# A fused attention and feed-forward kernel: two queues for a batch's stores, a divided last transpose, and another order of the last part's additions

## The chip, the cores and the metric

The kernel runs on one core of a Trainium2 chip. The metric is the device time of one execution in microseconds (us), given as the median of several executions of the same program. Beside these times stands one profiled execution, with a trace of every engine: PE (TensorE) does the matmuls and transposes, DVE (VectorE) and ACT (ScalarE) the element-wise work and the copies out of PSUM, POOL (GpSimd) little here, and SP only issues transfers (DMAs). ACT can issue transfers as well, from the same stream of instructions that holds its copies.

## The reference

Two steps. The first is attention whose mask comes from a hash; the second is a feed-forward layer with a parametric ReLU.

```python
# q, k, v: (4, 8, 768, 64); proj: (64, 6)
q_bucket = sum((q @ proj > 0) * 2**arange(6)); k_bucket = likewise
mask   = q_bucket[..., :, None] == k_bucket[..., None, :]
scores = where(mask, q @ k.T / sqrt(64), -1e9)
attn   = softmax(scores) @ v
x = attn.transpose(0, 2, 1, 3).reshape(3072, 512)
# moe_w_in: (512, 2048), moe_w_out: (2048, 512), moe_alpha: (2048,)
h = x @ moe_w_in
g = maximum(h, 0) + alpha * minimum(h, 0)
out = g @ moe_w_out            # (3072, 512) float32
```

## The kernel before

**Two paths.** `fast_path` computes everything under assumptions on the size of the inputs. `verdict()` tests these on the chip and writes an integer `flag`; after `fast_path` every engine reads the flag and branches over `general_path`, which is not run here (L401 and L402 in the profile, and L1245 for the program's closing waits).

**Stages.** The first third of the span is attention, unit by unit. After it come the feed-forward products for the four batches `b` = 0 to 3, as a list of 15 blocks per batch: eight blocks `ff1` (names `f_0` to `f_7`: x times w_in, with the parametric ReLU) and seven blocks `ff2` (names `z_p` for `p` in `ORDER = (1, 2, 5, 6, 3, 7, 4)`: the seven products of a fast matrix product of the Strassen kind that makes g times w_out). The result of `ff2` is in the tiles `m`, written `m_1` to `m_7` here; sums of them are the four parts of the batch's output, the parts 2, 3, 5 and 4 in the order in which they are ready.

**A block.** Each block is again seven small products, in the class `Product`. They go into three PSUM banks, a, b and c. `step(n)` emits one product and what follows it. Two products add into bank a after the bank was copied out, so that ACT's copy `keep` (L861 in the profile, tiles `..p` and `..u`) must have read the bank before PE writes it again. The four quarters of a block's result are "11", "12", "22" and "21"; `finish` puts each into the tile m: an addition on DVE (L990), or, for "21", a copy on ACT (L996). In block 4, the last of a batch, `finish` also adds `m_1`: for three quarters by a second addition (`add`, L984), for "21" by an addition straight from PSUM (L994).

**Order.** The order on every engine is the order in which the program emits the instructions; `do` keeps the compute instructions so, and each engine works through its own instructions in order. Around the end of a batch the block loop emits: the sums that prepare the next block's operands (`sum_g2`, L972, tile `gs`; `sum_w2`, L964, tile `ws`), `turn_out()`, then the next block's `step(1)`, and only then `step(4)` of the block at hand.

**Output.** The tiles `m` are transposed against the output. `turn_out` does this for finished parts: two DVE transposes of 32x32 blocks (L1014) into a tile `o`, then twelve stores of 32 KB each (L1020), all on SP's queue. For the two last parts of the last batch, `turn_last(0)` (part 5) and `turn_last(1)` (part 4) use PE transposes of 128x128 (L1036), which they call cells `(t, i)`: column block `t` of 3, row half `i` of 2. ACT copies them out of PSUM (L1041) and the stores are L1042: part 5 in one store on SP's queue, part 4 in two on ACT's. In part 4 the second store needs the quarter "21", which comes last.

**The verdict.** `largest()` leaves four maxima for each partition in the tile `top`. `verdict()` turns its four columns by four PE transposes into one row (L1056), reduces that row to four numbers (L1057), and computes the flag from them in seven small DVE instructions.

Of the kernel before, what the change touches and what calls it, by code (L numbers as in the profile page):

```python
# [8 lines left out]
F32 = mybir.dt.float32  # L9
# [3 lines left out]
ALU = mybir.AluOpType  # L13
# [335 lines left out]
def kernel(  # L349
# [48 lines left out]
    keep = ctx.enter_context(tc.tile_pool(name="keep", bufs=1))  # L398
    flag = keep.tile([1, 1], mybir.dt.int32, name="flag")
    fast_path(*args, flag)  # L400
    again = tc.nc.values_load(flag[0:1, 0:1])  # L401
    with tc.If(again > 0):  # L402
# [4 lines left out]
def fast_path(  # L407
# [12 lines left out]
    nc = tc.nc  # L420
    P = 128
    B, H, S, D = q.shape
# [8 lines left out]
    CH = 3  # L431
# [5 lines left out]
    SAFE = (40.0 / SCALE) ** 2  # L437
    EPS = 1e-30
    HI_MIN = 2.0 ** -15
    HI_END = 2.0  # L440

    do = tc.keep_in_program_order
    PE, DVE, ACT, POOL = nc.tensor, nc.vector, nc.scalar, nc.gpsimd

    const = ctx.enter_context(tc.tile_pool(name="const", bufs=1))
    dram = ctx.enter_context(tc.tile_pool(name="dram", bufs=1, space=bass.MemoryType.DRAM))
    mid = ctx.enter_context(tc.tile_pool(name="mid", bufs=2))
    psum = ctx.enter_context(tc.tile_pool(name="ps", bufs=1, space=bass.MemoryType.PSUM))
# [9 lines left out]
    ident = const.tile([P, P], F32, name="ident")  # L458
# [99 lines left out]
    order, left = [], [list(range(HW)), list(range(HW, NW))]  # L558
# [104 lines left out]
    def two_banks(name):  # L663
        return psum.tile([P, 2, 512], F32, name=name, tag="sc", bufs=3)
# [170 lines left out]
    class Product:  # L835

        def __init__(self, name, width, nk, left, right, finish):
            self.name, self.width, self.nk = name, width, nk  # L840
            self.left, self.right, self.finish = left, right, finish
            self.ps, self.sb = {}, {}

# [20 lines left out]
        def step(self, n):  # L864
            if n == 1:
                self.times("a", 0, 0, True)
                self.keep("a", "p1")
            elif n == 2:
                self.times("b", 1, 1, True)
            elif n == 22:  # L870
                self.finish("11", self.sb["p1"], self.ps["b"])
            elif n == 5:
                self.times("c", 3, 3, True)
                self.keep("c", "p5")
            elif n == 6:
                self.times("a", 4, 4, False)
                self.keep("a", "u1")
            elif n == 3:
                self.times("c", 6, 2, False)
                self.finish("12", self.sb["u1"], self.ps["c"])  # L880
            elif n == 7:
                self.times("a", 5, 5, False)
                self.keep("a", "u2")
                self.finish("22", self.sb["p5"], self.sb["u2"])
            elif n == 4:
                self.times("a", 2, 6, False)
                self.finish("21", self.ps["a"], None)
# [32 lines left out]
    H2, HK, HC = DM // 4, NI // 2, CW // 2  # L920
    w2, g2, m2, to_turn = {}, {}, {}, []
# [52 lines left out]
    def ff2(b, n):  # L974

        p = ORDER[n]
        acc = late[0].tile([P, 2, CW], F32, name=f"m{b}_{p}", tag={1: "m1", 5: "m5"}.get(p, "m"), bufs=1 if p in (1, 5) else 3)
        m2[b, p] = acc

        def add(to, x, *quarter):  # L980
            t, x = m2[b, to], m2[b, x]
            if quarter:
                t, x = (a[:, quarter[0], quarter[1] * HC : (quarter[1] + 1) * HC] for a in (t, x))
            do(DVE.tensor_tensor(t, t, x, op=ALU.add))  # L984

        def finish(c, x, more):
            i, jj = int(c[0]) - 1, int(c[1]) - 1
            dst = acc[:, i, jj * HC : (jj + 1) * HC]
            if more is not None:
                do(DVE.tensor_tensor(dst, x, more, op=ALU.add))  # L990
                if p == 4:
                    add(4, 1, i, jj)
            elif p == 4:
                do(DVE.tensor_tensor(dst, x, m2[b, 1][:, i, jj * HC : (jj + 1) * HC], op=ALU.add))  # L994
            else:
                do(ACT.copy(dst, x))  # L996
            if c == "21":

                for to, x in {2: [(2, 1)], 6: [(1, 6)], 3: [(3, 5), (3, 1)], 7: [(1, 7), (5, 1)]}.get(p, []):
                    add(to, x)  # L1000
                done = {2: (2, 0, 0), 3: (3, 0, 1), 7: (5, 1, 1), 4: (4, 1, 0)}.get(p)
                if done:
                    to_turn.append((b, *done))

        return Product(
            f"z{b}_{p}", HC, HK, lambda m, k: w2[b, n, m][:, k], lambda m, k: g2[b, n, m][:, k], finish,
        )

    def turn_out():
        while to_turn:  # L1010
            b, p, half, ch = to_turn.pop(0)
            o = late[0].tile([P, CW, 2], F32, name=f"o{b}_{p}", tag="o")
            for i in range(2):
                do(DVE.transpose(o[:, :, i], m2[b, p][:, i]))  # L1014

            src = o.rearrange("p (c w d) i -> p c w (d i)", c=CH, d=32)
            for a in range(DM // 128):
                for c in range(CH):
                    cols = slice(half * DM // 2 + 64 * a, half * DM // 2 + 64 * a + 64)
                    nc.sync.dma_start(  # L1020
                        out_v[b, ch * CH + c].rearrange("(w r) d -> r w d", r=32)[:, :, cols],
                        src[32 * a : 32 * a + 32, c],
                    )

    def turn_last(n):

        b, p, half, ch = to_turn.pop(0)
        o = late[0].tile([P, CH, P, 2], F32, name=f"o_{p}", tag=("o", "m5")[n], bufs=2 - n)
        dst = out_v[b, ch * CH : (ch + 1) * CH].rearrange("c p d -> p c d")[:, :, half * 2 * P : (half + 1) * 2 * P]
        goes = [([(t, i) for i in range(2) for t in range(CH)], slice(0, CH))]  # L1030
        if n:
            goes = [([(2, 0), (2, 1), (0, 0), (1, 0)], slice(2, CH)), ([(0, 1), (1, 1)], slice(0, 2))]
        for cells, ts in goes:
            ps = two_banks(f"to{p}").rearrange("p a f -> p (a f)").rearrange("p (i t f) -> p i t f", i=2, f=P)
            for t, i in cells:
                do(PE.transpose(ps[:, i, t], m2[b, p][:, i, t * P : (t + 1) * P], ident))  # L1036
            for i in range(2):
                t = [c[0] for c in cells if c[1] == i]
                if t:
                    t = slice(min(t), max(t) + 1)  # L1040
                    do(ACT.copy(o[:, t, :, i], ps[:, i, t]))  # L1041
            (nc.scalar if n else nc.sync).dma_start(dst[:, ts], o[:, ts].rearrange("p t f i -> p t (f i)"))  # L1042


    top = const.tile([P, 4], F32, name="top")
    row = const.tile([1, 4], F32, name="row")

    def largest():
        do(DVE.tensor_reduce(top[:, :2], mags, axis=mybir.AxisListType.X, op=ALU.max))
        do(DVE.tensor_reduce(top[:, 2:3], wmax, axis=mybir.AxisListType.X, op=ALU.max))  # L1050
        do(DVE.tensor_reduce(top[:, 3:4], alpha, axis=mybir.AxisListType.X, op=ALU.max))

    def verdict():
        ps = psum.tile([1, 4, P], F32, name="vd", tag="sm")
        for n in range(4):
            do(PE.transpose(ps[:, n], top[:, n : n + 1], ident))  # L1056
        do(DVE.tensor_reduce(row, ps, axis=mybir.AxisListType.X, op=ALU.max))  # L1057
        do(DVE.tensor_tensor(row[:, 0:1], row[:, 0:1], row[:, 1:2], op=ALU.mult))

        do(DVE.tensor_scalar(row[:, 0:1], row[:, 0:1], SAFE, None, op0=ALU.is_le))  # L1060
        do(DVE.tensor_scalar(row[:, 2:3], row[:, 2:3], HI_END, None, op0=ALU.is_lt))
        do(DVE.tensor_scalar(row[:, 3:4], row[:, 3:4], 1.0, None, op0=ALU.is_le))
        do(DVE.tensor_tensor(row[:, 0:1], row[:, 0:1], row[:, 2:3], op=ALU.mult))
        do(DVE.tensor_tensor(row[:, 0:1], row[:, 0:1], row[:, 3:4], op=ALU.mult))
        do(DVE.tensor_scalar(flag, row[:, 0:1], -1.0, 1.0, op0=ALU.mult, op1=ALU.add))

# [89 lines left out]
    late = []  # L1158
# [7 lines left out]
    for j, (b, what, n) in enumerate(blocks):  # L1166
# [10 lines left out]
        if j == 4:  # L1177
            largest()
# [30 lines left out]
        if j + 1 < len(blocks):  # L1209
            turn_out()  # L1210
        else:
            turn_last(0)
        before = now
        if j + 1 < len(blocks):
            b1, what1, n1 = blocks[j + 1]
            now = ff1(b1, n1) if what1 == "1" else ff2(b1, n1)
            now.step(1)
        before.step(4)
        if n2 < 7:
            sum_g2(b, n2, 6)  # L1220
    turn_last(1)
# [1 line left out]
_INS = ['q', 'k', 'v', 'proj', 'moe_w_in', 'moe_w_out', 'moe_alpha']  # L1223
# [26 lines left out]
```

## Time and profile before

| what | value |
|---|---|
| median of 8 runs | 903.73 us (903.01 to 906.18) |
| the profiled execution | 902.53 us |
| its span, first to last instruction | 900.7 us |
| mean granted TensorE clock | 0.998 |
| PE busy | 887.1 us (98%) |
| DVE busy | 754.8 us (84%) |
| ACT busy | 408.6 us (45%) |
| PE's weight loads busy | 591.8 us (66%) |
| last matmul ends | about 893.5 us |
| last store issued | 894.53 us |

The profiled execution lies 1.8 us over its own span, and 1.20 us under the median of the eight runs. Times inside the trace count from the span's start. A line of the timeline gives the start, the length, the engine, the line of the kernel, the operation with its tiles (numbers left out) and, in brackets, how long the engine was idle before it and for what. PEld is PE's weight load; SPq and ACTq are the queues' own rows, here mostly the issuing of transfers, whose data moves later. Consecutive instructions of one kind are merged into one row.

### The profile page before, as it was taken

What the parts mean: (1) busy time and instruction counts of PE and PEld (TensorE: products, weight loads), DVE (VectorE), ACT (ScalarE), POOL (GpSimd) and SP (SyncE); (2) the same over time, 40 slices, a digit from 0 to 9 for tenths busy, and PEclk for the clock granted to TensorE, in tenths of its full rate; (3) what the DMA queues carried; (4) which work ended last, traced back from release to release, by engine and by line L of the source; (5) the groups of instructions that cost most, each with busy time, mean ns of one, the idle gap of its engine ahead of it and who ended that gap; (6) DMA issues with size and microseconds to landing.
All of it is one profiled execution on the core that took longest, in us unless ns stands there. A gap on an engine that the chain in (4) does not pass through costs nothing.

```text
span 900.7 us, 15654 instructions
## 1 busy us (share of the span) xinstructions
PE 887.1 (98%) x5885; PEld 591.8 (66%) x5885; DVE 754.8 (84%) x1353; ACT 408.6 (45%) x733; POOL 100.4 (11%) x194
## 2 busy tenths in 40 slices
PE   8999999999999999999999999999999999999996
PEld 4444445444444445556997557998557998556996
DVE  4888988988998996799889668989768989768985
ACT  7888888888888863222112222112222111222111
POOL 1222222222222232120000000000000000000000
PEclk9999999999999999999999999999999999999999
DMA  8778888698798665478343525242525242521242
GB/s 228 185 187 183 208 226 212 164 274 232 167 244 207 175 163 187 150 248 298 135 154 86 183 85 190 94 158 81 188 83 192 95 158 76 192 83 41 95 143 72
DMA packets 131909, 146.88 MB, mean 163 GB/s; under 512 B 78304, under 2 KB 118000, under 8 KB 128240
## 3 DMA queue, kind: packets, MB, share of 16 engines
q1 hardware_dynamic: 118800, 124.03, 44.6%
q0 software_dynamic: 11008, 20.97, 11.5%
q8 instruction: 48, 0.79, 0.4%
q10 hardware_dynamic: 2016, 0.79, 0.3%
q14 instruction: 37, 0.30, 0.1%
HBM read 104.87 MB, written 28.31 MB: 148 GB/s over the span
## 4 chain that ended last, share of the span: by engine, by line
PE 94%; DVE 2%; DMA 2%; ACT 1%; issue 0%; ACTq 0%
PE sc L734 17%; PE av L767 14%; PE f_0a L854 2%; PE f_2a L854 2%; PE f_5a L854 2%; PE z_4a L854 2%; PE z_5a L854 2%; PE z_6a L854 2%; PE z_7a L854 2%; PE z_3a L854 2%; PE f_3a L854 2%; PE z_2a L854 2%; PE f_6a L854 2%; PE f_4a L854 2%; PE f_1a L854 2%; PE z_1a L854 2%
## 5 line engine op out<-in xcount | busy, mean ns | idle before, releaser
L739 ACT ACTIVATE pt<-sc 128x768 f32<-128x768 f32 x192 | 152.8, 814 | 46.7 <-PE sc L734 44.4
L734 PE MATMUL sc<-qT,kT 64*128 64x384 f32 x768 | 155.3, 483 | 0.0
L767 PE MATMUL av<-pt,vn 128*32 128x384 f32 (+1 forms) x1536 | 130.7, 488 | 0.0
L767 PEld LDWEIGHTS av<-pt,vn 128*32 128x32 f32 x1536 | 46.8, 110 | 74.9 <-issue 72.7
L734 PEld LDWEIGHTS sc<-qT,kT 64*128 64x128 f32 x768 | 68.3, 188 | 35.0 <-issue 34.8
L904 DVE TENSOR_TENSOR g<-g,g 128x384 f32<-128x384 f32 x128 | 68.4, 555 | 2.2
L734 PE MATMUL sc<-qb,kb 64*128 64x384 bf16 x384 | 63.4, 325 | 1.9 <-ACT kb L722 1.0
L749 POOL DMA_DIRECT2D accp<-pt x32 | 38.6, 1205 | 190.9 <-issue 86.0
L972 DVE TENSOR_TENSOR gs<-g,gs 128x768 f32<-128x768 f32 x56 | 53.4, 953 | 1.0
L964 DVE TENSOR_TENSOR ws<-wl 128x512 f32<-128x512 f32 x56 | 38.5, 688 | 17.7 <-DMA wl<-w_out_s 16.4
L972 DVE TENSOR_TENSOR gs<-g 128x768 f32<-128x768 f32 x56 | 53.3, 952 | 0.0
L900 DVE SCALAR_TENSOR_TENSOR g<-h,alpha 128x384 f32<-128x384 f32 x32 | 19.7, 617 | 27.2 <-ACT h L893 27.2
L734 PEld LDWEIGHTS <-kb 64*128 64x128 bf16 x384 | 19.4, 94 | 33.1 <-issue 11.1
L711 ACT ACTIVATE qb<-hs,hb 32x384 bf16<-32x384 f32 x62 | 35.5, 573 | 1.1
L757 DVE TENSOR_TENSOR accd<-accd,accp 128x768 f32<-128x768 f32 x32 | 30.7, 958 | 4.5 <-DMA accp<-pt 3.5
L754 DVE TENSOR_TENSOR accd<-accd,pt 128x768 f32<-128x768 f32 x32 | 30.7, 959 | 3.3
L748 DVE TENSOR_TENSOR accp<-pt,pt 128x768 f32<-128x768 f32 x32 | 30.4, 951 | 2.5 <-ACT pt L739 2.5
L753 DVE TENSOR_TENSOR accd<-pt,pt 128x768 f32<-128x768 f32 x32 | 30.4, 949 | 0.0
L803 POOL COPY rr<-rr 32x6 f32<-32x6 f32 x64 | 27.6, 431 | 2.6
L984 DVE TENSOR_TENSOR m<-m,m 128x768 f32<-128x768 f32 (+1 forms) x36 | 27.1, 752 | 0.7
L722 ACT ACTIVATE kb<-hs,hb 64x384 bf16<-64x384 f32 (+1 forms) x47 | 27.1, 577 | 0.6
L802 POOL COPY rr<-rr 32x6 f32<-32x6 f32 x64 | 19.9, 310 | 65.2 <-DVE rr L799 63.9
(336 smaller groups left out, 1806.7 us busy)
## 6 DMA issues: line engine op xcount, KB each, us to landing
wi<-w_in_s SPq DMA_DIRECT2D x32, 896.0 KB, 4.8
wl<-w_out_s SPq DMA_DIRECT2D x16, 1024.0 KB, 4.8
accp<-pt POOLq DMA_DIRECT2D x32, 384.0 KB, 5.4
wl<-w_out_r SPq DMA_DIRECT2D x12, 1024.0 KB, 4.8
raw<-in_moe_w_out_dram SPq DMA_DIRECT2D x16, 512.0 KB, 5.6
raw<-in_moe_w_in_dram SPq DMA_DIRECT2D x16, 512.0 KB, 5.1
w_in_s<-wsi SPq DMA_DIRECT2D x16, 448.0 KB, 5.8
vn<-in_v_dram SPq DMA_DIRECT2D x16, 384.0 KB, 5.9
```

What stands on the lines that cost most here:

```text
L711: do(ACT.activation(bits["q", pi][D * s : D * s + 32, cols], ps["q"][c : c + 32, half, :CW], AF.Sign, bias=hb[c : c + 32],))
L734: do(PE.matmul(sc[:, s, :CW], what["k", pi][r, ks], what["q", pi][r, qs], start=first, stop=not first,))
L739: do(ACT.activation(pt[:, :, :CW], sc[:, :, :CW], AF.Exp, scale=SCALE / DOWN))
L748: do(DVE.tensor_tensor(accp[u], p(u, 0), p(u, 1), op=ALU.add))
L749: nc.gpsimd.dma_start(accp[u], p(u, 2), accum_op=ALU.add)
L754: do(DVE.tensor_tensor(accd[u], accd[u], p(u, 5), op=ALU.add))
L757: do(DVE.tensor_tensor(accd[u], accd[u], accp[u], op=ALU.add))
L767: do(PE.matmul(av[u][D * s + t : D * s + t + 32, :w], nat["v", pi][:, s, kc * D + t : kc * D + t + 32], prob[u, kc][:, s, :w], start=(kc = ...
L854: do(PE.matmul(self.ps[bank], self.left(left, k), self.right(right, k), start=start and k == 0, stop=k == self.nk - 1, skip_group_check=no ...
L904: do(DVE.tensor_tensor(new_g(b, to)[:, i], g_m[b, x][:, i], g_m[b, y][:, i], op=ALU.subtract))
L964: do(DVE.tensor_tensor(t, w2[b, n, x], w2[b, n, y], op=op))
L972: do(DVE.tensor_tensor(t, g2[b, n, x], g2[b, n, y], op=ALU.subtract))
```

## The change

It has four parts.

1. The twelve stores of part 3 in the last batch are divided: the four with an odd `c` are issued by ACT, the other eight stay with SP.
2. In block 4 of each batch, `m_1` is added to the kept copies (`p1`, `p5`, `u1`) by a new function `kept` that `step(22)` and `step(6)` call, ahead of the `finish` that adds the rest. The number of additions is the same, seven for a block; in the quarters "12" and "22" other instructions come between the two.
3. `turn_last(0)` takes two PSUM tiles of three transposes instead of one of six. `turn_last(1)` takes three PSUM tiles of two transposes: DVE copies the first (`tx`) and the last (`tz`), ACT the second (`ty`); the part that ACT copies is stored by ACT, the other two thirds by SP, in one store after the last copy.
4. `verdict()` turns all four columns by one PE transpose, reduces over the four partitions, and brings the four numbers into one row by a DVE transpose of 32x32, for which `largest()` first clears a tile.

```diff
         def step(self, n):
...
             elif n == 22:
+                self.kept("11", self.sb["p1"])
                 self.finish("11", self.sb["p1"], self.ps["b"])
...
             elif n == 6:
                 self.times("a", 4, 4, False)
                 self.keep("a", "u1")
+                self.kept("22", self.sb["p5"])
+                self.kept("12", self.sb["u1"])
...
         def finish(c, x, more):
             i, jj = int(c[0]) - 1, int(c[1]) - 1
             dst = acc[:, i, jj * HC : (jj + 1) * HC]
-            if more is not None:
+            if p == 4:
+                do(DVE.tensor_tensor(dst, m2[b, 1][:, i, jj * HC : (jj + 1) * HC] if more is None else dst, x if more is None else more, op=ALU.add))
+            elif more is not None:
                 do(DVE.tensor_tensor(dst, x, more, op=ALU.add))
-                if p == 4:
-                    add(4, 1, i, jj)
-            elif p == 4:
-                do(DVE.tensor_tensor(dst, x, m2[b, 1][:, i, jj * HC : (jj + 1) * HC], op=ALU.add))
             else:
                 do(ACT.copy(dst, x))
...
+        def kept(c, x):
+            i, jj = int(c[0]) - 1, int(c[1]) - 1
+            m = m2[b, 1][:, i, jj * HC : (jj + 1) * HC]
+            do(DVE.tensor_tensor(acc[:, i, jj * HC : (jj + 1) * HC], x, m, op=ALU.add))
...
     def turn_out():
...
-                    nc.sync.dma_start(
+                    (nc.scalar if b == B - 1 and p == 3 and c % 2 else nc.sync).dma_start(
                         out_v[b, ch * CH + c].rearrange("(w r) d -> r w d", r=32)[:, :, cols],
                         src[32 * a : 32 * a + 32, c],
                     )
...
     def turn_last(n):
...
-        for cells, ts in goes:
-            ps = two_banks(f"to{p}").rearrange("p a f -> p (a f)").rearrange("p (i t f) -> p i t f", i=2, f=P)
-            for t, i in cells:
-                do(PE.transpose(ps[:, i, t], m2[b, p][:, i, t * P : (t + 1) * P], ident))
...
+        if n == 0:
+            o = late[0].tile([P, CH, P, 2], F32, name=f"o_{p}", tag="o")
+            for i in range(2):
+                do(ACT.copy(o[:, :, :, i], cells(f"to{i}", [(t, i) for t in range(CH)])))
+            nc.sync.dma_start(dst, o.rearrange("p t f i -> p t (f i)"))
+            return
+        o = late[0].tile([P, 2, P, 2], F32, name=f"o_{p}", tag="o")
+        o2 = late[0].tile([P, P, 2], F32, name=f"o2_{p}", tag="m5", bufs=1)
+        ps = cells("tx", [(0, 0), (1, 0)])
+        ps2 = cells("ty", [(2, 0), (2, 1)])
+        do(DVE.tensor_copy(o[:, :, :, 0], ps))
+        do(ACT.copy(o2.rearrange("p f i -> p i f"), ps2))
+        nc.scalar.dma_start(dst[:, 2], o2.rearrange("p f i -> p (f i)"))
+        do(DVE.tensor_copy(o[:, :, :, 1], cells("tz", [(0, 1), (1, 1)])))
+        nc.sync.dma_start(dst[:, :2], o.rearrange("p t f i -> p t (f i)"))
...
     def largest():
+        do(DVE.memset(col, 0.0))
...
     def verdict():
-        ps = psum.tile([1, 4, P], F32, name="vd", tag="sm")
-        for n in range(4):
-            do(PE.transpose(ps[:, n], top[:, n : n + 1], ident))
-        do(DVE.tensor_reduce(row, ps, axis=mybir.AxisListType.X, op=ALU.max))
+        ps = psum.tile([4, P], F32, name="vd", tag="sm")
+        do(PE.transpose(ps, top, ident))
+        do(DVE.tensor_reduce(col[:4, 0:1], ps, axis=mybir.AxisListType.X, op=ALU.max))
+        do(DVE.transpose(row, col))
...
```

The helper `cells(name, at)` of the new `turn_last` makes one PSUM tile and puts the transposes of the list `at` side by side into it. In the built program the tiles `tx` and `ty` reuse the banks of the two tiles of part 5, and `tz` the bank a of block `z_4`.

More of the change, by code (lines that the diff above doesn't have):

```diff
@@ L835, in fast_path, with __init__ @@
     class Product:
-        def __init__(self, name, width, nk, left, right, finish):
+        def __init__(self, name, width, nk, left, right, finish, kept=None):
             self.name, self.width, self.nk = name, width, nk
+            self.kept = kept if kept else lambda c, t: None
             self.left, self.right, self.finish = left, right, finish
@@ L1003, in finish @@
                     to_turn.append((b, *done))
+        def kept(c, x):
+            i, jj = int(c[0]) - 1, int(c[1]) - 1
+            m = m2[b, 1][:, i, jj * HC : (jj + 1) * HC]
+            do(DVE.tensor_tensor(acc[:, i, jj * HC : (jj + 1) * HC], x, m, op=ALU.add))
         return Product(
             f"z{b}_{p}", HC, HK, lambda m, k: w2[b, n, m][:, k], lambda m, k: g2[b, n, m][:, k], finish,
+            kept if p == 4 else None,
         )
@@ L1027, in turn_last, with cells @@
         b, p, half, ch = to_turn.pop(0)
-        o = late[0].tile([P, CH, P, 2], F32, name=f"o_{p}", tag=("o", "m5")[n], bufs=2 - n)
         dst = out_v[b, ch * CH : (ch + 1) * CH].rearrange("c p d -> p c d")[:, :, half * 2 * P : (half + 1) * 2 * P]
-        goes = [([(t, i) for i in range(2) for t in range(CH)], slice(0, CH))]
-        if n:
-            goes = [([(2, 0), (2, 1), (0, 0), (1, 0)], slice(2, CH)), ([(0, 1), (1, 1)], slice(0, 2))]
-        for cells, ts in goes:
-            ps = two_banks(f"to{p}").rearrange("p a f -> p (a f)").rearrange("p (i t f) -> p i t f", i=2, f=P)
-            for t, i in cells:
-                do(PE.transpose(ps[:, i, t], m2[b, p][:, i, t * P : (t + 1) * P], ident))
-            for i in range(2):
[L1038 to L1042, printed above, removed]
+        def cells(name, at):
+            ps = two_banks(f"{name}{p}")[:, 0].rearrange("p (t f) -> p t f", f=P)
+            for k, (t, i) in enumerate(at):
+                do(PE.transpose(ps[:, k], m2[b, p][:, i, t * P : (t + 1) * P], ident))
+            return ps[:, : len(at)]
@@ L1045, in fast_path @@
+        ps2 = cells("ty", [(2, 0), (2, 1)])
[4 more added lines that the diff above has]
+        nc.sync.dma_start(dst[:, :2], o.rearrange("p t f i -> p t (f i)"))
     top = const.tile([P, 4], F32, name="top")
-    row = const.tile([1, 4], F32, name="row")
+    col = const.tile([32, 32], F32, name="col")
@@ L1048, in largest @@
+    row = const.tile([32, 32], F32, name="row")
     def largest():
+        do(DVE.memset(col, 0.0))
         do(DVE.tensor_reduce(top[:, :2], mags, axis=mybir.AxisListType.X, op=ALU.max))
@@ L1053, in verdict @@
     def verdict():
-        ps = psum.tile([1, 4, P], F32, name="vd", tag="sm")
-        for n in range(4):
-            do(PE.transpose(ps[:, n], top[:, n : n + 1], ident))
-        do(DVE.tensor_reduce(row, ps, axis=mybir.AxisListType.X, op=ALU.max))
[L1058 to L1065, printed above, removed]
+        ps = psum.tile([4, P], F32, name="vd", tag="sm")
+        do(PE.transpose(ps, top, ident))
+        do(DVE.tensor_reduce(col[:4, 0:1], ps, axis=mybir.AxisListType.X, op=ALU.max))
+        do(DVE.transpose(row, col))
+        do(DVE.tensor_tensor(row[0:1, 0:1], row[0:1, 0:1], row[0:1, 1:2], op=ALU.mult))
+        do(DVE.tensor_scalar(row[0:1, 0:1], row[0:1, 0:1], SAFE, None, op0=ALU.is_le))
+        do(DVE.tensor_scalar(row[0:1, 2:3], row[0:1, 2:3], HI_END, None, op0=ALU.is_lt))
+        do(DVE.tensor_scalar(row[0:1, 3:4], row[0:1, 3:4], 1.0, None, op0=ALU.is_le))
+        do(DVE.tensor_tensor(row[0:1, 0:1], row[0:1, 0:1], row[0:1, 2:3], op=ALU.mult))
+        do(DVE.tensor_tensor(row[0:1, 0:1], row[0:1, 0:1], row[0:1, 3:4], op=ALU.mult))
+        do(DVE.tensor_scalar(flag, row[0:1, 0:1], -1.0, 1.0, op0=ALU.mult, op1=ALU.add))
     last = UNITS - 1
```

## The prediction

> **What bounds the kernel now.** I read the page's chain first, then PE's waits, then the timeline of the last 15 us, and last the DMA view, the events behind the branch and the windows. The chain says that the matmuls are the path:
>
> ```profile
> PE 94%; DVE 2%; DMA 2%; ACT 1%; issue 0%; ACTq 0%
> ```
>
> PE is busy 98% of the span and its longest single wait is 1.4 us for a weight load (f_2a). So an edit counts only if it lets PE start a product earlier or later, or if it lies behind the last product. The stretch that decides, from the timeline:
>
> ```profile
> 882.77 0.32 ACT L861 COPY z_4p<-z_4a 128x192 f32<-128x192 f32 x1 [0.97 <-PE z_4a L854]
> 884.02 0.32 ACT L996 COPY m<-z_7a 128x192 f32<-128x192 f32 x1 [0.94 <-PE z_7a L854]
> 886.26 1.33 PEld L854 LDWEIGHTS z_4a<-gs,ws 128*128 128x128 f32 x8
> 886.34 1.03 DVE L1014 STREAM_TRANSPOSE o<-m 128x384 f32<-128x384 f32 x2
> 887.29 1.91 DVE L984 TENSOR_TENSOR m<-m,m 128x768 f32<-128x768 f32 x2
> 887.40 5.56 SPq L1020 DMA_DIRECT2D out_dram<-o  x12
> 890.98 1.55 PE L854 MATMUL z_4a<-gs,wl 128*128 128x192 f32 x8
> 892.56 0.36 DVE L994 TENSOR_TENSOR m<-z_4a,m 128x192 f32<-128x192 f32 x1 [0.51 <-PE z_4a L854]
> 893.07 0.41 PE L1036 MATMUL to<-ident,m 128*128 128x128 f32 x2
> 893.70 0.37 ACTq L1042 DMA_DIRECT2D out_dram<-o  x1
> 894.11 0.38 ACT L1041 COPY o<-to 128x256 f32<-128x256 f32 x1 [0.44 <-ACT o L1041]
> 894.53 0.39 ACTq L1042 DMA_DIRECT2D out_dram<-o  x1
> ```
>
> Columns: start, length, engine, line, operation, and idle time before it. PE runs without a gap up to 892.53. Behind it: the last add (892.92), two transposes (893.48), a copy that waits 0.6 us behind ACT's own store issue, and the last store, issued at 894.53. The DMA view has 4.0 us to landing for the 128 KB store (893.70 to 897.7), 3.8 for the 256 KB one (894.53 to 898.33), and 3.5 for SP's 384 KB:
>
> ```profile
> out_dram<-o SPq DMA_DIRECT2D x1, 384.0 KB, 3.5
> out_dram<-o ACTq DMA_DIRECT2D x1, 256.0 KB, 3.8
> out_dram<-o ACTq DMA_DIRECT2D x1, 128.0 KB, 4.0
> ```
>
> After its last store an engine reads the flag, branches over the general path and reaches the closing waits. DVE waits for nothing of others there, and still needs 3.2 us:
>
> ```profile
> L402 DVEq COMPARE_BRANCH  x1: 72/72/72, 893.2 to 893.2; - x1
> L402 SPq COMPARE_BRANCH  x1: 45/45/45, 894.1 to 894.1; - x1
> L402 DVEq EVENT_SEMAPHORE  x1: 21/21/21, 896.5 to 896.5; - x1
> L402 SPq EVENT_SEMAPHORE  x8: 17/17/17, 897.7 to 898.7; - x8
> ```
>
> SP's eight waits are for the stores; the span ends 2.4 us after the last landing (898.33 to 900.74).
>
> **Part 1: four stores of part 3 on ACT's queue.** The order of instructions puts them on ACT behind z_7's last copy (ended 881.8) and before the copy of z_4a's first product (L861, 882.77), the copy of z_7a's last quarter into m_7 (L996, 884.02) and everything later. They wait for the DVE transposes L1014, which end at 887.37. That a waiting or issuing store holds the copies behind it is in the rows: the copy at 894.11 had its transposes at 893.48 and began only when the store of 893.70 was issued. The DVE work up to 887.37 needs nothing of the held copies, so those transposes keep their time.
>
> So ACT stands from 881.8 to 887.40 and then issues four stores. SP's twelve of the same shape take 5.56 us, 0.463 each: 1.85 us, to 889.25. Bounds: 4 x 0.315 = 1.26 (shortest row of the shape) and 2.20 (the four loads that ACT issues at the start, with three times as many pieces). I take 1.85 for its equal shape. Then comes the first copy, 0.32, to 889.57.
>
> PE's product z_4a<-gs,ws at 886.26 adds into the bank that this copy reads, so it waits for the copy. With 0.08 for the signal (the last add ends at 892.92, the weight load it frees starts at 893.04; a DMA landing at 389.40 frees one at 389.44) its first weight load comes at 889.65 instead of 886.26: **PE is 3.4 us late**, 2.8 to 3.75 by the bounds. PE has no slack after that.
>
> What is late next? ACT's m_7 copy ends at 889.8; DVE's two adds L984 follow (1.83 from start to next start, to 891.65), then gs for the last product (to 892.55). PE, shifted, wants m_5 at 893.56 and that gs at 894.35: 1.8 us of slack. Six adds at 0.33 behind it end near 894.6, before the shifted last quarter at 895.96. So nothing beyond 3.4 us is added there. SP is relieved of 4 x 0.463 = 1.85 us, which brings nothing: its 384 KB store is then set by the ACT copies, issued about 895.2, landed about 898.7, well ahead of the last.
>
> [...]
>
> **Part 2: the quarters added ahead.** Seven adds before, seven after, each 0.33 to 0.36. At the end DVE idles 0.51 us before the last quarter's add anyway, and that add starts when PE's last product ends: 0. In batches 0 to 2 the bank z_4c is read one add later (482.01 to about 482.35), z_4b likewise (481.35 to 481.7); the next block's products in these banks load weights at 485.95 and 484.82. That 3 us is the cover; without it each would cost 0.35 us, three times.
>
> **Part 3: the last part's end.** With S for PE's delay: the last pair of transposes ends at 893.48+S as before, and now DVE copies it at once. A DVE copy of 128x256 lies between the 192-wide add (0.35) and the 384-wide copy from PSUM (L678, 0.558): 0.42. The SP store goes out at 893.98+S instead of 894.53: -0.55. Landing takes 3.5 to 3.8: another 0 to -0.3. That store's wait stands later in SP's list of waits than the old one, so less of the list is left behind it: -0.2. If the landing ends the kernel, the end gives -0.75 to -1.05.
>
> But now SP issues last. Store 0.40, flag read and branch 0.66: the branch is done at 895.04+S. Then the way to the waits, which before took SP at most 3.6 us (894.12 to 897.72), DVE 3.2 and ACT 2.8 (895.85 to 898.62): first wait at 897.84+S to 898.64+S. From the first wait unhindered: eight waits 0.6, closing 1.97. End at 900.41+S to 901.21+S, against 900.74: -0.33 to +0.47. The later of the two ends counts, so the end gives -0.85 to +0.47; I take -0.1, as three engines' rows say that the branch costs 2.8 us or more.
>
> **Part 4: the verdict.** PE saves three transposes of 0.11 each, but f_5a's first weights load at 389.44 because wi landed at 389.40: 0. On DVE a 0.67 reduction gets shorter, a small memset and a 32x32 transpose are added: -0.4 to +0.2 on an engine for which PE does not wait there; taken as 0.
>
> **Sum.** 3.4 - 0.1 = +3.3 us. The profiled execution took 902.53 (span 900.7), so 905.8 for such a one; the median of the eight runs lies 1.20 above it: **907.0 us**, 0.37% slower. About 0.2%, 1.8 us, is what a measurement of this kernel can tell from no change.
>
> **The rivals.**
> *The clock falls in the gap.* PE would stand from 886.43 to 889.65, 3.2 us. At the kernel's end the granted clock falls after as short a time: the last matmul ends at 893.48, and
>
> ```profile
> 896.00:897.00 1.00, 0.00 (x0) 0.00 (x0) 0.00 (x0) 0.00 (x0) 0.00 (x0) 0.68 0.41 129
> 897.00:898.00 1.00, 0.00 (x0) 0.00 (x0) 0.00 (x0) 0.00 (x0) 0.00 (x0) 0.50 0.08 28
> ```
>
> (the number before the DMA share is PEclk): 0.68 over that window is full speed up to 896.37, 2.9 us after. At the start transposes take 0.42 until about 5.5 us, where the first matmul began at 1.20, and 0.27 later: 4.3 us to recover, half of it lost, about 2.1 us. Against it: no gap of this trace reaches 2.9 us with work behind it. Time: 907.0 + 2.1 = 909.1. Chance 0.18. [...]
>
> *The stores cost PE nothing.* If the copy of z_4a ran before the stores, S = 0 and the end alone remains: -0.1 to -0.85 us, 903.3. The order on ACT and the held copy at 894.11 speak against it. Chance 0.10, and this is no change.
>
> *Faster by over 1.8 us.* Everything behind PE's last product to the last landing is 5.8 us, 3.8 of it the landing itself; it would need S = 0 and a saving twice the end's best bound. Chance 0.04.
>
> Forecast as summed: 0.68. Slower holds it and the clock: 0.86.
>
> **The range.** Lowest of the forecast: 2.8 - 0.85 - 0.4 = +1.55, 905.3; highest 3.75 + 0.47 + 0.2 = +4.4, 908.1. To hold eight in ten it must take in most of the clock's case: 905.2 to 909.2.
>
> **What would show it.** ACT idle from about 881.8 to 887.4, then four ACTq stores of about 0.46, then three copies back to back; PE idle about 3.2 us before z_4a<-gs,ws, released by ACT z_4p; DVE's m add waiting for ACT; the last transposes near 896.9; SP's last store near 897.4 and its first closing wait about 4 us later; PEclk 1.0 in 886 to 896 (or 0.5 if the first rival holds); f_5a still released by the load of wi. If PE has no gap there, the main step is wrong; if the gap is there and the span is not 2.5 us or more longer, the end was mis-sized.

## The result

The changed kernel took 908.27 us (median of 12 runs, 906.9 to 910.54) against 903.95 for the kernel before beside it (32 runs): a ratio of 1.0047, interval 1.0036 to 1.0058, so 4.25 us more (3.3 to 5.2). The forecast was 907.0, that is +3.3, with 905.2 to 909.2 as its range.

The profiled execution after took 908.84 us, its span 907.05 against 900.74. Of these 6.3 us, 2.7 arise 500 us ahead of the changed stretch: in this one execution the loads of w_in (`wi`) for f_2a, f_5a and f_7a let PE wait 3.0, 2.0 and 1.8 us instead of 2.0, 0.4 and 1.5. Such waits differ about as much without any edit, as the sixth experiment shows (f_2a 3.7 us). So stretches are compared here with each other, not starts in the trace.

### The profile page after: what moved, and what is told of

Its sections match the earlier page's. It is cut to its first block, busy times and chain, and to the rows that moved or that the text cites. A ratio compares the mean times of both kernels' runs of the same rounds, so it can differ in the third digit from the quotient of the medians.

```text
span 907.0 us, 15657 instructions
## 1 busy us (share of the span) xinstructions
PE 887.5 (98%) x5882; PEld 591.7 (65%) x5882; DVE 754.9 (83%) x1357; ACT 407.8 (45%) x731; POOL 100.5 (11%) x194
## 4 chain that ended last, share of the span: by engine, by line
PE 91%; DMA 5%; DVE 1%; SPq 1%; issue 0%; ACTq 0%; ACT 0%; POOL 0%; DVEq 0%; POOLq 0%
PE sc L734 17%; PE av L767 14%; PE z_2a L855 2%; PE f_0a L855 2%; PE f_5a L855 2%; PE f_2a L855 2%; PE z_3a L855 2%; PE z_6a L855 2%; PE z_5a L855 2%; PE f_3a L855 2%; PE z_4a L855 2%; PE f_6a L855 2%; PE f_1a L855 2%; PE f_4a L855 2%; PE z_7a L855 2%; PE z_1a L855 2%
## 5 line engine op out<-in xcount | busy, mean ns | idle before, releaser
L855 PE MATMUL f_2a<-x,wi 128*128 128x384 f32 x64 | 23.4, 488 | 2.4 <-DMA wi<-w_in_s 2.4
```

Source lines behind the costliest of these rows:

```text
L855: do(PE.matmul(self.ps[bank], self.left(left, k), self.right(right, k), start=start and k == 0, stop=k == self.nk - 1, skip_group_check=no ...
```

## The profile after

The chain of waits of the changed kernel shows that the matmuls are still the path, with a larger share of transfers than the 2% before (47 us, of which 17 are two loads of `wi`):

```profile
PE 91%; DMA 5%; DVE 1%; SPq 1%; issue 0%; ACTq 0%; ACT 0%; POOL 0%; DVEq 0%; POOLq 0%
```

The timeline of the stretch that decides (start, length, engine, line, operation, idle time before it; L862 is the old L861, L1023 the old L1014, L1030 the old L1020, L988 the old L984; L995 adds the last quarter, L1057 and L1060 are DVE's copies of `tx` and `tz`, L1061 is SP's last store):

```profile
889.05 1.03 DVE L1023 STREAM_TRANSPOSE o<-m 128x384 f32<-128x384 f32 x2
890.11 3.69 SPq L1030 DMA_DIRECT2D out_dram<-o  x8
890.12 1.85 ACTq L1030 DMA_DIRECT2D out_dram<-o  x4
892.07 0.32 ACT L862 COPY z_4p<-z_4a 128x192 f32<-128x192 f32 x1 [7.57 <-DMA out_dram<-o]
...
892.44 1.27 PEld L855 LDWEIGHTS z_4a<-gs,ws 128*128 128x128 f32 x8 [3.45 <-ACT z_4p L862]
...
892.64 1.95 DVE L988 TENSOR_TENSOR m<-m,m 128x768 f32<-128x768 f32 x2 [2.55 <-ACT m L999]
...
897.10 1.55 PE L855 MATMUL z_4a<-gs,wl 128*128 128x192 f32 x8
898.68 0.35 DVE L995 TENSOR_TENSOR m<-m,z_4a 128x192 f32<-128x192 f32 x1 [1.23 <-PE z_4a L855]
899.08 0.43 DVE L1057 COPY o<-tx 128x256 f32<-128x256 f32 x1
...
899.57 0.42 DVE L1060 COPY o<-tz 128x256 f32<-128x256 f32 x1
900.02 0.40 SPq L1061 DMA_DIRECT2D out_dram<-o  x1
```

The reader sees the predicted picture line by line. ACT stands for 7.57 us until its four stores are issued (1.85 us); the releaser is given as the store, but the rows above it say what the store itself waited for: the DVE transposes. At once the copy of z_4a follows, and PE's weight load, which used to come without a wait, is 3.45 us late. DVE's adds L988 are late too, but the last product, at 897.10, has no wait in front of it: the delay is passed on and does not grow.

Behind the last product the DMA view has

```profile
out_dram<-o SPq DMA_DIRECT2D x1, 256.0 KB, 3.8
out_dram<-o ACTq DMA_DIRECT2D x1, 128.0 KB, 1.8
```

and the events behind the branch (L402) and at the program's end (L1266):

```profile
L402 SPq EVENT_SEMAPHORE  x8: 17/17/17, 901.5 to 904.0; - x8
L402 DVEq COMPARE_BRANCH  x1: 72/72/72, 900.2 to 900.2; - x1
L402 SPq COMPARE_BRANCH  x1: 45/45/45, 901.0 to 901.0; - x1
L402 DVEq EVENT_SEMAPHORE  x1: 21/21/21, 903.8 to 903.8; - x1
```

```profile
L1266 ACTq EVENT_SEMAPHORE  x2: 17/17/17, 905.5 to 907.0; - x2
L1266 DVEq EVENT_SEMAPHORE  x2: 21/21/21, 906.7 to 907.0; - x2
```

SP reaches its first wait 0.45 us after its branch (901.07 to 901.52), not 2.8 to 3.6 us after it. So the landing, at 903.81, holds SP's list and not the branch. But DVE comes to its closing wait at 906.7, 1.2 us after ACT at 905.5, and everything waits for it. Before, all came together:

```profile
L1245 ACTq EVENT_SEMAPHORE  x2: 17/17/17, 900.1 to 900.7; - x2
L1245 DVEq EVENT_SEMAPHORE  x2: 21/21/21, 900.1 to 900.7; - x2
```

## The experiments

"Gap" is how long PE's weight load for z_4a<-gs,ws stood; "behind PE" is the time from the end of the last product to the end of the span. A time given as a difference is the ratio's, with its interval, times 904 us.

### The four stores back on SP

```diff
-                    (nc.scalar if b == B - 1 and p == 3 and c % 2 else nc.sync).dma_start(
+                    nc.sync.dma_start(
```

> The changed kernel with part 1 alone undone: all twelve stores of part 3 on SP's queue again. Theory W (ACT's copies are held behind stores that wait for DVE, and PE behind the first of these copies): the gap of 3.45 us before z_4a's second product is gone, its weight load follows the one of z_4c without a gap, and the time falls by 3.5 us against the changed kernel, to 904.8, within 1 us of the kernel before. Theory K (the other three parts cost it, by their additions, their copies or their transposes): it stays at 907 to 908, whatever becomes of the gap. By the prediction's own sum the rest of the change should be worth -0.1 us against the kernel before.

Measured: 905.6 us, ratio 1.0011 (0.9997 to 1.0025). No gap. The loss is mostly gone, so part 1 makes most of it. Whether anything remains the times don't tell (-0.3 to +2.3 us), but the timeline of this kernel has a place for it:

```profile
896.69 0.43 DVE L1057 COPY o<-tx 128x256 f32<-128x256 f32 x1 [1.22 <-DMA out_dram<-o]
```

DVE's first copy of the last part waits for a landing. In `turn_last(1)` the new tile `o` shares the memory of part 3's `o`, from which SP's twelve stores still read. Last product to last store issued takes 2.39 us here, against 1.37 with four stores on ACT and 2.00 in the kernel before. So parts 1 and 3 are tied: in this trace, without part 1, part 3's last store goes out later where it should go out sooner.

### Part 1 alone

```diff
-                    nc.sync.dma_start(
+                    (nc.scalar if b == B - 1 and p == 3 and c % 2 else nc.sync).dma_start(
```

The edit is to the kernel before.

> The kernel before with part 1 alone done. Theory W: PE stands 3.4 to 3.5 us before z_4a's second product, released by ACT's first copy of z_4a, and the time rises by 3.4 to 3.5 us to 907.4; the end behind PE's last product stays as before (8.2 us). Theory K: within 1 us of the kernel before.

Measured: 909.22 us (5 runs), ratio 1.0053 (1.004 to 1.0067): +4.8 us (3.6 to 6.1), with a gap of 3.31 us. Part 1 alone makes the whole loss, and about 1.5 us more than its gap. The timeline has the gap as PE's matmuls see it, and the windows of this kernel show where the rest may come from (behind PE, PEld, DVE, ACT and POOL: the granted clock, the DMA share, GB/s):

```profile
890.50 1.91 PE L854 MATMUL z_4a<-gs,ws 128*128 128x192 f32 x8 [3.01 <-ACT z_4p L861]
```

```profile
891.00:892.00 1.00, 1.00 (x7) 1.00 (x6) 0.97 (x2) 0.00 (x0) 0.00 (x0) 0.79 0.34 72
892.00:893.00 1.00, 1.00 (x5) 1.00 (x4) 1.00 (x2) 0.32 (x1) 0.00 (x0) 0.50 0.26 54
```

The clock halves at 891.58, after PE has restarted, for 3.41 us. The stretch from the start of z_4a's second product, the first after the gap, to the end of the last takes 7.88 us. In the changed kernel's first trace, whose clock stays full, it takes 6.20.

### The four stores on ACT, but later

ACT's four stores are collected and emitted in the last block after `step(6)`, behind the copies that PE and DVE wait for. All else is as in the changed kernel.

```diff
-                    (nc.scalar if ... else nc.sync).dma_start(...)
+                    if b == B - 1 and p == 3 and c % 2:
+                        later.append(store)
+                    else:
+                        store(nc.sync)
...
             now.step(6)
+            if j + 1 == len(blocks):
+                for store in later:
+                    store(nc.scalar)
             now.step(3)
```

> The changed kernel with the same four stores still on ACT's queue, but emitted behind the last block's step(6), so that ACT has made its copies p1, m_7 and p5 before the first of them. Theory W: the stores find the DVE transposes done or nearly done, there is no gap before z_4a's second product, and the time is that of the kernel with all stores on SP's queue (904.8). Rival Q (two queues that issue at once, or stores on ACT's queue as such, cost it): 2 us or more stay, 906.5 to 908.3, with slow issues of 0.9 us or late landings in the trace.

Measured: 904.2 us, ratio 0.9997 (0.9989 to 1.0006). In the timeline the first of the four is now issued at 888.54, between copies:

```profile
888.54 0.38 ACTq L1033 DMA_DIRECT2D out_dram<-o  x1
889.16 1.31 ACTq L1033 DMA_DIRECT2D out_dram<-o  x3
```

There is no gap, and the last store goes out 1.37 us after PE's last product, as in the changed kernel. The same stores on the same queue cost nothing in another place: it is the place in ACT's order that costs, not the second queue, nor the four issues as such.

### One store of twelve on ACT

```diff
-... p == 3 and c % 2 else nc.sync).dma_start(
+... p == 3 and c % 2 and a == 0 else nc.sync).dma_start(
```

> The changed kernel with one store of the twelve on ACT's queue instead of four. Theory W splits the 3.45 us into a wait for the DVE transposes, paid once, and 0.463 us for each store issued: the gap before z_4a's second product is 3.45 - 3 x 0.463 = 2.06 us, the time 906.9. If the cost were in the number of stores (rival Q), the gap would be a quarter, 0.9 us, and the time 905.7.

Measured: 906.61 us, ratio 1.0018 (1.0006 to 1.0031), +1.6 us. Its timeline:

```profile
888.22 0.38 ACTq L1030 DMA_DIRECT2D out_dram<-o  x1
...
889.07 1.27 PEld L855 LDWEIGHTS z_4a<-gs,ws 128*128 128x128 f32 x8 [2.00 <-ACT z_4p L862]
```

The gap of 2.00 us separates the delay's two terms: most of the 3.45 is the wait for the transposes, which one store brings as fully as four. The other three issues add 1.45. No clock fall shows behind it: the next eight matmuls take 1.57 us, as in the changed kernel's first trace.

### Parts 2 and 4 alone

The edit is to the kernel before: the additions and the verdict as changed, `turn_out` and `turn_last` as before.

```diff
+                self.kept("11", self.sb["p1"])
...
+        ps = psum.tile([4, P], F32, name="vd", tag="sm")
+        do(PE.transpose(ps, top, ident))
```

> The kernel before with parts 2 and 4 alone (the additions ahead, the one turn for the verdict); stores and last transposes as before. The prediction's step says 0 for both: within 0.5 us of the kernel before, PE without a gap at the ends of the batches, f_5a's first weights released by the load of wi, the end behind PE's last product 8.2 us. Theory K (these parts cost something): 1 us or more slower, with a wait of PE that the kernel before does not have, at f_5a or at the first products of batches 1 to 3.

Measured: 904.21 us, ratio 0.9996 (0.9987 to 1.0004): nothing. In the changed kernel's trace the verdict's one reduction takes 0.27 us instead of 0.67, and f_5a still waits for the load of `wi`, as forecast.

### The kernel before, a second time

No edit.

> The kernel before, unchanged, as another sample of what differs from run to run: ratio 1.000, and in its trace other lengths than before of the waits for the loads of wi and wl (f_2a 2.0, f_5a 0.4, f_7a 1.5, z_2a 0.6 us in the first trace), since these vary by 1 to 3 us among the traces of the first four experiments at places that no edit touches. If they come out the same again, these waits belong to the edits and not to the run.

Measured: 905.02 us, ratio 1.0003 (0.9994 to 1.0013). Its profiled span is 904.73, 4.0 us longer than the first trace of the same program: f_2a waited 3.7 us in all for loads, and the clock halved at 363.71, behind that wait, for 3.41 us. This is the size of what one trace can say of a whole span.

### ACT makes all the last copies

As with the later stores, but ACT makes the copies of `tx` and `tz` too, and its own store comes after SP's.

```diff
-        do(DVE.tensor_copy(o[:, :, :, 0], ps))
+        do(ACT.copy(o[:, :, :, 0], ps))
         do(ACT.copy(o2.rearrange("p f i -> p i f"), ps2))
-        nc.scalar.dma_start(dst[:, 2], ...)
-        do(DVE.tensor_copy(o[:, :, :, 1], cells("tz", ...)))
+        do(ACT.copy(o[:, :, :, 1], cells("tz", ...)))
         nc.sync.dma_start(dst[:, :2], ...)
+        nc.scalar.dma_start(dst[:, 2], ...)
```

> As the kernel with the four stores emitted later (e3), but all three copies of part 4's end are made by ACT, so that DVE ends with the last quarter's addition; SP stores two thirds, ACT its third behind the last copy. Theory D (DVE's own way from its branch to the program's last waits takes some 6.5 us and sets the end where DVE has the last copy): from PE's last product to the end 7.5 to 7.6 us instead of 8.4, and the last landing is followed by about 2.1 to 2.4 us instead of 3.5; the time is 0.6 us under the kernel before. Theory L (the last landing sets the end): 8.3 to 8.4 as in e3, as the last store goes out at the same time.

Measured: 903.53 us, ratio 0.999 (0.998 to 1.0001). The last store leaves 1.33 us after the last product, as early as with DVE's copies. So DVE's copies were not needed for the early store. DVE's late closing wait is gone here, for a reason that this kernel alone doesn't tell: DVE ends earlier, and its program is three instructions shorter.

### DVE kept busy at the end, with two and with five additions

To the kernel before, additions are put at the end of DVE's work; their result is not used.

```diff
     turn_last(1)
+    extra = late[0].tile([P, 2, CW], F32, name="extra", tag="m", bufs=3)
+    for i in range(2):
+        do(DVE.tensor_tensor(extra, m2[B - 1, 1], m2[B - 1, 1], op=ALU.add))
```

> The kernel before with two additions of 128x768 more on DVE behind the last quarter's addition, whose result nobody reads: DVE reaches its branch 1.8 us later, the stores go out as before. Theory D: the end moves from 8.2 to 9.3 us behind PE's last product (branch at 2.55, and 6.5 us, and 0.3), the time rises by 1.1 us. Theory L: the end stays 8.2 us behind PE's last product.

Measured: 904.85 us, ratio 1.0003 (0.9993 to 1.0014). It decides nothing: the last landing took 4.41 us in its trace, and hid whatever DVE did. So the same with five additions, in one execution:

> As the kernel before with more additions on DVE behind the last quarter's, but five instead of two (4.4 us instead of 1.8), so that the two theories of the end no longer fall together: in the run with two the last store took 4.4 us to land, and landing and DVE came out at the same time. Theory D: DVE's branch 5.1 us behind PE's last product, 6.4 to 6.5 us more to its first closing wait, 0.35 to the end: 11.9 us. Theory L: 8.2 to 9.1 us as in the other traces with these stores.

Measured: one execution of 905.82 us, against 904.39 before. Behind PE it took 9.30 us, not 11.9. DVE branched at 899.13 and reached its closing wait with the others, 3.7 us later. In the changed kernel it needs 6.5 us (900.2 to 906.7). So DVE's lateness there is no fixed time that its way to the end always takes.

### The changed kernel a second time

No edit.

> The changed kernel again, for a second trace: the gap before z_4a's second product 3.4 to 3.5 us again, as order and issue times set it; the waits for wi and wl of other lengths than in the first trace, as they vary from run to run; the end 8.4 us behind PE's last product, with DVE's first closing wait 1.2 to 1.5 us behind those of the other engines if theory D holds. Granted clock 1.0 up to PE's last product, or half of it for some us behind the gap if the prediction's clock rival strikes in this run.

Measured: one execution of 910.01 us. The gap is 3.54 us, and now the clock halves inside it, at 889.80, for 6.83 us. From the windows and the timeline of this second trace:

```profile
889.00:890.00 1.00, 0.00 (x0) 0.00 (x0) 0.00 (x0) 0.00 (x0) 0.00 (x0) 0.90 0.28 63
...
892.00:893.00 1.00, 1.00 (x5) 1.00 (x4) 0.97 (x2) 0.00 (x0) 0.00 (x0) 0.50 0.31 71
```

```profile
891.03 2.93 PE L855 MATMUL z_4a<-gs,ws 128*128 128x192 f32 x8 [3.25 <-ACT z_4p L862]
```

Eight matmuls take 2.93 us; in the first trace of the same program they take 1.57. The stretch from z_4a's second product on is 8.95 us long instead of 6.20.

### ACT's copies, a second time

No edit to that kernel.

> The version with the stores emitted later and all last copies on ACT (e7) again, for a second sample of its ratio: 0.999 of the kernel before, 0.2 to 1.0 us less; the end 7.5 to 8.1 us behind PE's last product, by the time that the last store takes to land (3.4 to 4.4 us in the traces so far), without a late DVE.

Measured: 903.15 us, ratio 0.9994 (0.9982 to 1.0007). With the first time (0.999), no gain that can be told from no change.

### More code on DVE

The kernel with the later stores, and in `largest()` the tile `col` is cleared 17 times instead of once, 500 us before the end.

```diff
-        do(DVE.memset(col, 0.0))
+        for i in range(17):
+            do(DVE.memset(col, 0.0))
```

> The version with the stores emitted later and DVE's two copies at the end (e3), with sixteen more clearings of the small verdict tile on DVE in the middle of the kernel, where it has slack. In five traces DVE reaches its first closing wait 0.6 to 1.5 us behind the other engines; all five programs have 2660 instructions on DVE, and the eight traces without it have 2651 to 2657. Theory C (the late wait hangs on where DVE's closing code lies in its program): with 2676 it is gone, DVE comes with the others, the landing is followed by 2.1 to 2.4 us instead of 3.5, and from PE's last product to the end it takes 7.2 to 7.6 us by the same landing. Theory D (it hangs on DVE's having the last copy): DVE is late by 1.2 to 1.5 us as before, 8.4 us from PE's last product.

Measured: 905.24 us, ratio 1.0006 (0.9996 to 1.0016). The closing events of the kernel with the later stores, and then of this one:

```profile
L1274 DVEq DRAIN  x2: 17/18/18, 899.0 to 901.9; - x2
L1274 ACTq EVENT_SEMAPHORE  x2: 17/17/17, 900.2 to 902.0; - x2
L1274 DVEq EVENT_SEMAPHORE  x2: 21/21/21, 901.8 to 902.1; - x2
```

```profile
L1275 DVEq DRAIN  x2: 10/14/17, 899.0 to 900.9; - x2
L1275 ACTq EVENT_SEMAPHORE  x2: 17/17/17, 900.8 to 901.4; - x2
L1275 DVEq EVENT_SEMAPHORE  x2: 21/21/21, 900.8 to 901.4; - x2
```

In the first, DVE comes 1.5 us after ACT; with 16 more small instructions, far away, both come at 900.8, and the time from the last landing to the end is 2.31 us instead of 3.54. Part of that is the landing itself, which took 4.17 us here and 3.51 there and so makes the others later. But DVE gets from its DRAIN, the instruction ahead of its closing wait, to that wait in at most 1.8 us (899.0 to 900.8) instead of 2.8 (899.0 to 901.8). DVE's work at the end is the same in both. The lateness is gone, as theory C forecast; that it hangs on where DVE's closing code lies in its program, one trace of each does not show. The times have no sign of it: one microsecond is too little for them.

## Why the prediction held, and where it did not

**The delay of PE: right.** Forecast 3.4 us (2.8 to 3.75); measured 3.45, 3.31 and 3.54 in three traces. Its terms held one by one: four issues 1.85 us, the copy 0.32, the stores released as the transposes end (ended about 890.1, issued from 890.12). The signal took 0.05 instead of 0.08. Nothing further was late, as the slack of 1.8 us said. The single store confirms the split of the sum. Putting the same stores later removes it all.

**The additions and the verdict at 0: right**, within -1.2 to +0.4 us.

**The end: its size right by luck, its steps wrong.** Forecast -0.1 (-0.85 to +0.47), measured +0.2: 8.40 us behind PE instead of 8.21. The forecast had a landing side, -0.75 to -1.05, and a side where SP's way behind its branch ends last. The landing side came: the last store goes out 0.63 us sooner, and its landing took 3.79 us as before. Had DVE come with the others at 905.5, and had the rest taken 0.6 us as before (900.1 to 900.7), the end would stand at about 7.4 us, -0.8. The step that failed is SP's branch. I had put it at 2.8 us or more from three engines' rows, and SP took 0.45. SP's own row of before, 3.6 us, was no price of the branch: its first wait ended at 897.72, as the 128 KB store landed at 897.70. In the trace after, DVE took 3.6 us from its branch to its first wait (900.2 to 903.8) and ACT 3.7 (900.5 to 904.2); why SP takes less, no run shows. What ate the gain was something that no row of before could show, DVE's late closing wait (the third column is the time from DVE's DRAIN to its closing wait; where DVE is not late, it is only an upper bound of what DVE needs):

| kernel | DVE's instructions | DVE's DRAIN to closing wait, us | DVE late at the closing, us | last landing to end, us | behind PE, us |
|---|---|---|---|---|---|
| before | 2651 | 3.5 | not seen | 2.41 | 8.21 |
| after | 2660 | 2.75 | 1.2 | 3.23 | 8.40 |
| after, second trace | 2660 | 2.4 | 0.6 | 2.61 | 8.24 |
| stores on SP | 2660 | 2.2 | 0.7 | 2.67 | 8.50 |
| stores later | 2660 | 2.8 | 1.5 | 3.54 | 8.42 |
| one store | 2660 | 2.8 | 1.35 | 3.31 | 8.52 |
| part 1 alone | 2651 | 2.7 | not seen | 1.84 | 7.29 |
| parts 2 and 4 | 2657 | 3.4 | not seen | 2.41 | 8.52 |
| ACT's copies, two traces | 2657 | 2.5, 2.2 | not seen | 2.33 | 8.06, 7.85 |
| before with five additions | 2656 | 0.65 | not seen | 3.35 | 9.30 |
| more code on DVE | 2676 | 1.8 | not seen | 2.31 | 7.85 |

All five traces with 2660 instructions have it, and none of the others. But where DVE has 2.2 us or more between the two, a stall as long as in the five (2.2 to 2.8 us) need not be seen; only the two traces with 0.65 and 1.8 us leave no room for it. In the DMA view of the first trace after, three packets of the row `q14 instruction`, about 8 KB each (37 of them make 0.30 MB in the whole execution), lie between DVE's DRAIN and its closing wait (904.0 to 906.7). But they do not name their engine, and the kernel before, where DVE is not late, has three there as well (896.6 to 900.1), so the cause stays open.

**SP's relief "brings nothing": wrong in the background.** Without it, the copy of `tx` waits for part 3's stores (DVE idle for 1.22 us with the stores on SP). The sum wasn't touched, as the forecast took both parts together, but I had not seen that `turn_last(1)` now uses part 3's tile.

**The clock: a rival that was part of the result.** I gave it 0.18 as a case apart, with +2.1 us. The traces show it after two gaps of three, at +1.7 us (gap 3.01) and +2.75 us (gap 3.25), and not after the gap of 3.15. The mean granted clock that is listed with each execution points the same way for many more: 0.9957 over the 20 executions of the changed kernel and of part 1 alone, 0.9970 over 108 of the kernel before, those beside the experiments and those of the sixth. A clock of 0.996 or less was seen in 12 of the 20 and in 25 of the 108. The difference, 0.0013 of 905 us, is 1.2 us of full-speed time; the part of it that falls into the gap itself costs nothing. So an estimate of about 1 us from the clock, 3.45 of delay and an end of about 0 come near the 4.25 us measured (3.3 to 5.2), and lie within the interval of part 1 alone (3.6 to 6.1). The estimate is rough: each mean also holds a half clock at the program's end, 4.4 us in the first trace of the kernel before and 2.7 in the first after, and the means of the kernel before ran from 0.9962 (12 executions) to 0.9973 (15). The step that failed is the chance: it should have been a term of the sum, of some 1 us or more, and not an unlikely case. I had gone by the length of the gap alone; by these three gaps, the length alone does not tell.

**The other rivals** fell: the stores did cost PE, and the kernel is not faster.

Open remain: what makes DVE late; and what sets the last landing, which took 3.4 to 4.4 us for much the same store in these traces. That range alone is as large as all that part 3 could win.

## What to carry to other kernels

Here the transfers that ACT issued waited in ACT's order, and held every copy behind them for 7.57 us. So before moving a store to a compute engine's queue, look up when its data is ready, and who waits for the copies behind it. Emitted behind those copies, they cost nothing that could be measured here (1.0047 turned into 0.9997). And where an edit makes a busy PE stand, reckon with a half clock as a possible part of the price (here 1.7 and 2.75 us with gaps of 3.01 and 3.25 us, nothing with one of 3.15).

## What was not expected of the hardware

**The clock fell with short waits, and not with every one.** PE stood 3.25 us in the second trace of the changed kernel and 3.01 us with part 1 alone, and the clock halved both times; with the stores on SP it halved at 428.80 after PE stood 1.97 us for a load of `wl`, and in the second run of the kernel before at 363.71, after 2.47 us for `wi`. In the first trace after, 3.15 us did not trip it, nor did 2.4 us for `wi` at f_2a. The half clock lasted 3.41 us in three of the four, and 6.83, twice that, in the second trace of the changed kernel. The length of a wait alone does not tell in these traces whether the clock falls.

Its place may. The full clock that ends with the fall behind the last matmul lasted 890.88 us in the first trace of the kernel before and 897.71 us in the first after, which is 261 and 263 times 3.413 us, the length of the half clock above. So I counted how long PE's matmuls stood in stretches of 3.413 us, laid end to end through the full clock of these two traces, leaving out gaps under 0.15 us. Up to PE's last matmul it is at most 1.32 us in the one and 1.72 us in the other, and the clock stayed full. In the 3.413 us ahead of each of the four falls it is 1.97 (stores on SP), 2.02 (second trace of the changed kernel), 2.26 (second run of the kernel before) and 2.33 us (part 1 alone). The 3.15 us that did not trip the clock, from 889.29 to 892.44, were divided by the end of a stretch at 890.72, four of them ahead of the fall at 904.37, into 1.43 and 1.72 us. So the clock fell in these traces where PE stood 1.97 us or more in one stretch, and stayed where it stood 1.72 us or less; no run varies this alone. An estimate from these numbers, with the border taken halfway, at 1.85 us: a gap of 3.0 to 3.25 us escapes only if the end of a stretch falls into the middle 0.45 to 0.7 us of it. If the stretches may lie anywhere, that puts the chance of a fall at 0.8 or somewhat more, where the prediction had 0.18.

**DVE's closing wait came sooner with more instructions ahead.** With 16 small instructions more on DVE, 500 us earlier, DVE went from its DRAIN to its closing wait in at most 1.8 us instead of 2.8. This rests on one trace of each kernel, and what moved it was not shown.
